# A second buffer for the tiles that the DMA turns, and v's loads, squares and parts moved between blocks

## The chip, the cores and the metric

The kernel runs on one core of a Trainium2 chip. The metric is the device time of one execution in microseconds (us), given as the median of several runs. An engine is named as in the profile: PE multiplies, ACT (ScalarE) and DVE (VectorE) work on whole tiles, POOL does one addition per pair of heads, and SP issues nearly all DMAs from one queue, in order.

## What is computed

Attention with a sigmoid in place of the softmax for 8 batches of 12 heads (448 tokens, 64 numbers per head), and behind it a two-layer network on the 3584 tokens:

```python
scores = scale * np.matmul(q, k.transpose(0, 1, 3, 2)) - np.log(S)
attn = 1.0 / (1.0 + np.exp(-scores))
attn_out = np.matmul(attn, v)
x = attn_out.transpose(0, 2, 1, 3).reshape(B * S, H * D)
h = x @ w_in
g = h - np.tanh(h)
return g @ w_out
```

## The kernel before

**Number format.** From batch 1 on, q and k, and from batch 2 on v and the sigmoids too, are split into two float16 parts, high and low, after a scaling by a power of two; a product is then three PE passes (high-high, high-low, low-high). The scaling needs the sum of squares of q, k and v for two pairs of heads: `norm` (lines 311 to 316) squares a tile on ACT and adds it up, throwing the squares into a junk tile of tag "sq"; `scales` (lines 318 to 345) makes the factors.

**Two stages per batch.** For each batch the first layer (`moe1`, line 746) is a dense run of PE products. The second layer (`moe2`, line 855) has 48 steps of 6 products (line 874) over three token tiles of 128 (16 steps each), then a rest of 64 tokens (line 912). Between its steps the attention of the next batch is fed in, in blocks, by the numbers in `BLOCKS` (8, 12, 16, ... 52): after that many steps, one block. At the end of a token tile (steps 16, 32, 48) the two accumulators leave PSUM, one on ACT (line 903, tile `o`), one on DVE (line 904). There are two PSUM buffers for them, so PE can't begin the next token tile before both are copied out.

**The blocks.** `stream` (lines 450 to 611) yields four blocks per two pairs of heads, g and h = g + 1:
- block 1 (lines 574 to 583): the first two score tiles of g, the products attention times v (`do_av`) of the pair before, v's parts of h (`prep_v(h)`), the loads of q and k of g+3 and of v of g+3, and the squares of v of g+2;
- block 2 (585 to 591): the remaining score tiles of g, the split of their sigmoids (`keep`, which calls `split_a`, lines 399 and 400), the squares of q, k and v of g+3;
- block 3 (593 to 599): the factors for g+2 and g+3, the first score tiles of h, and the parts of k and q of g+2 (`parts_k`, `parts_q`);
- block 4 (601 to 609): the last score tile of h, the parts of k and q of g+3, v's parts of g+2, the load of v of g+4, and the squares of q and k of g+4.

With `BLOCKS`, block 4 comes at steps 8, 24 and 40, block 1 at 12, 28 and 44, block 2 at 16, 32 and 48, right behind the evacuation of a token tile, and block 3 at 20, 36 and 52.

**The turned tiles.** `parts` (lines 347 to 361) writes the two float16 parts of k or q into a tile `w` (line 351) and has the DMA turn it into `K` or `Q` (line 358, issued on SP). For q the high part is written by ACT (line 353) and the low part by DVE (line 356); for k both are written by DVE (lines 355 and 356). `w` has one buffer: whoever writes the next `w` waits for the DMA that reads the one before. In the order of the program the four `w` of two pairs are k of g+2, q of g+2, k of g+3, q of g+3.

**What sets the order.** The order of PE, ACT, DVE and POOL is that in which the code is written. The DMAs on SP are put in order by a scheduler, which may issue a load ahead of the place where the code asks for it. Each engine takes its instructions in order, so one that waits holds up all behind it.

**The staged weights.** While w_in is converted at the start, `conv_norm` (line 159) writes squares of its pieces into tiles of tag "sq" of which four are in flight, and `conv_end` (line 170) sums four at a time on PE.

Of the kernel before, what the change touches and what calls it, by code (L numbers as in the profile page):

```python
# [8 lines left out]
F16 = mybir.dt.float16  # L9
BF16 = mybir.dt.bfloat16  # L10
# [9 lines left out]
P = 128  # L20
D = 64
CK = 112
# [12 lines left out]
class Builder:  # L35
# [123 lines left out]
    def conv_norm(self, p):  # L159
        nc = self.nc  # L160
        k = p["k"]
        if not p["staged"]:
            return
        p["sq"] = self.sm.tile([P, p["piece"][3]], BF16, name="sq", tag="sq", bufs=4)
        if k % 6 == 1:
            nc.vector.scalar_tensor_tensor(p["sq"], p["F"], 1.0, p["F"], op0=ALU.mult, op1=ALU.mult)
        else:
            nc.scalar.activation(p["sq"], p["F"], AF.Square)
# [142 lines left out]
    def norm(self, t, out):  # L311

        flat = t.rearrange("p a b d -> p (a b d)" if len(t.shape) == 4 else "p a d -> p (a d)")
        rows, n = flat.shape
        junk = self.sm.tile([P, 8 * D], BF16, name="sqn", tag="sq", bufs=4)
        self.nc.scalar.activation(junk[:rows, :n], flat, AF.Square, accum_out=out[:rows])  # L316

    def scales(self, ss, where):
# [28 lines left out]
    def parts(self, n, s, name, act):  # L347

        nc = self.nc
        flat = n.rearrange("p c h d -> p (c h d)")  # L350
        w = self.qk.tile([CK, 2, 4 * P], F16, name="w", tag="w", bufs=1)
        if act:
            nc.scalar.activation(w[:, 0], flat, AF.Copy, scale=s[:CK])  # L353
        else:
            nc.vector.tensor_scalar(w[:, 0], flat, s[:CK], None, op0=ALU.mult)
        nc.vector.scalar_tensor_tensor(w[:, 1], flat, s[:CK], w[:, 0], op0=ALU.mult, op1=ALU.subtract)  # L356
        o = self.qk.tile([P, 2, self.S], F16, name=name, tag=name)
        nc.sync.dma_start_transpose(
            o.rearrange("p x (c t) -> p (x c) t", c=4), w.rearrange("p x e -> p (x e)")
        )  # L360
        return o
# [88 lines left out]
    def stream(self):  # L450

        NP = self.NP
        G = (self.B - 1) * NP
        at = lambda g: (1 + g // NP, g % NP)
        splits = lambda g: at(g)[0] >= self.AV32
        qk, vn, sc, K, Q, vv, accs = {}, {}, {}, {}, {}, {}, {}

        def load(g):
            if g < G and g not in qk:
                qk[g] = self.load_qk(*at(g))

        def load_v(g):
            if g < G and splits(g):
                vn[g] = self.load_v(*at(g), self.nat, "vn", 2)

        def sums(g):
            ss = self.sums[g // 2 % 2]  # L470
            return ss if splits(g) else ss[:, :4]

        def norms(g):
            if g < G:
                for n, t in enumerate(qk[g]):
                    self.norm(t, sums(g)[:, 2 * n + g % 2 : 2 * n + g % 2 + 1])

        def norm_v(g):
            if g in vn:
                self.norm(vn[g], sums(g)[:, 4 + g % 2 : 5 + g % 2])  # L480

        def scales(g, where):
            if g < G:
                sc[g] = sc[g + 1] = self.scales(sums(g), where)

        def parts_k(g):
            if g < G:
                K[g] = self.parts(qk[g][0], sc[g][0][:, 0:1], "K", not splits(g) and g not in (2, 3))

        def parts_q(g):  # L490
            if g < G:
                Q[g] = self.parts(qk[g][1], sc[g][0][:, 1:2], "Q", True)
                qk.pop(g)

        def prep_v(g):
            if g >= G:
                return
            if splits(g):
                vv[g] = self.prep_v(vn.pop(g), sc[g][0])
            else:  # L500
                vv[g] = self.load_v(*at(g), self.att, "vhl", 3)[:, None]

        load(0)
        load(1)
        yield 0, False
        norms(0)
        norms(1)
        yield 0, False
        scales(0, "tr")
        parts_k(0)  # L510
        yield 450, False
        parts_q(0)
        load(2)
        yield 450, False
        parts_k(1)
        yield 450, False
        parts_q(1)
        load(3)
        yield 450, False
        norms(2)  # L520
        yield 0, False
        todo = []

        def open_acc(g):
            tag = "tr" if g % 2 else "av"
            accs[g] = self.ps.tile([P, 512], F32, name="acc", tag=tag, bufs=1)
            if g % NP == 0:
                self.xs = []

        def close_acc(g):  # L530
            iv = sc[g][1][:, 1:2] if splits(g) else None
            self.xs.append(self.evac_x(g % NP, accs.pop(g), iv))
            if g % 2:
                vv.pop(g - 1)
                vv.pop(g)
            for d in (sc, K, Q):
                d.pop(g)

        def do_av():
            for g, c, A in todo:  # L540
                odd = g % 2
                if c == QT:
                    open_acc(g + 1)
                    self.av([accs[g], accs[g + 1]], vv[g], A, c, odd)
                    close_acc(g)
                    continue
                if c == 0 and not odd:
                    open_acc(g)
                self.av([accs[g]], vv[g], A, c, odd)
                if c == QT - 1 and odd:  # L550
                    close_acc(g)
            todo.clear()

        def units(g, cs, between=lambda: None):

            pss = []
            for c in cs:
                n = 2 if c == QT else 1
                pss.append(self.scores([K[g + i] for i in range(n)], [Q[g + i] for i in range(n)], c))
            aa = [self.weigh(pss[0], sc[g][1][:, 0:1])]  # L560
            between()
            aa += [self.weigh(ps, sc[g][1][:, 0:1]) for ps in pss[1:]]
            return aa

        def keep(g, cs, aa):
            if splits(g):
                aa = [self.split_a(a) for a in aa]
            todo.extend((g, c, a) for c, a in zip(cs, aa))

        for g in range(0, G, 2):  # L570
            h = g + 1
            early = not splits(g)

            aa = units(g, (0, 1))
            do_av()
            if g == 0:
                prep_v(0)
            prep_v(h)
            keep(g, (0, 1), aa)
            load(g + 3)  # L580
            load_v(g + 3)
            norm_v(g + 2)
            yield 2750, True

            aa = units(g, (2, QT))
            if early:
                do_av()
            keep(g, (2, QT), aa)
            norms(g + 3)
            norm_v(g + 3)  # L590
            yield 2750, True

            scales(g + 2, "sc" if early else "av")
            aa = units(h, (0, 1), lambda: parts_k(g + 2))
            do_av()
            keep(h, (0, 1), aa)
            parts_q(g + 2)
            load(g + 4)
            yield 2750, True

            aa = units(h, (2,), lambda: parts_k(g + 3))
            if early:
                do_av()
            keep(h, (2,), aa)
            parts_q(g + 3)
            prep_v(g + 2)
            load_v(g + 4)
            norms(g + 4)
            yield 2750, True
        do_av()  # L610
        yield 1150, True
# [454 lines left out]
```

## Time and profile before

| | |
|---|---|
| time, median of 3 runs | 1353.88 us (1351.56 to 1355.76) |
| profiled execution, its own time | 1343.7 us |
| its span, from first to last instruction | 1341.4 us |
| mean granted PE clock | 0.958 of full speed |
| ACT busy, DVE busy | 902.5 us (67%), 910.6 us (68%) |
| SP's DMA queue, share of 16 DMA engines | 27.6% |

A row of a timeline gives the start of an instruction (or of several alike, "x24") in us from the beginning of the span, how long it lasted, its engine, its line, what it writes and reads, and in brackets how long the engine had stood idle before it and what ended that. A row of "windows" gives for a stretch of time how long each engine was busy in it and which share of the full PE clock was granted. A matmul's end is modelled, so a PE that is shown as busy can still run at a lower clock. Batch 3's second layer, with the attention of batch 4 in it, lies between 673.5 and 773.7 us; the other batches look alike, but the last has no attention to feed in, and the one before it less.

### The profile page before, as it was taken

How to read it: one execution, taken by the hardware profiler on the slowest of the kernel's cores; microseconds unless marked ns; L12 is line 12 of the kernel's file. 1: busy time of each engine (PE TensorE's matmuls, PEld its weight loads, DVE VectorE, ACT ScalarE, POOL GpSimd, SP SyncE). 2: the span in 40 equal slices, each digit the busy share in tenths (PEclk: the TensorE clock that was granted, in tenths of full speed). 3: DMA queues.
4: the chain of work that ended last, by engine and by line, in shares of the span. 5: the costliest groups of instructions: out<-in, count | busy, mean ns of one | idle time of the engine just before them, and what ended most of it. 6: DMA issues, size and time to landing. Idle time of an engine off the chain costs nothing.

```text
span 1341.4 us, 19713 instructions
## 1 busy us (share of the span) xinstructions
PE 1220.2 (91%) x7633; PEld 622.4 (46%) x7633; DVE 910.6 (68%) x1376; ACT 902.5 (67%) x1262; POOL 37.9 (3%) x38
## 2 busy tenths in 40 slices
PE   9899767799888899889998899888998999899998
PEld 3244323355444455445544455444544455445555
DVE  5999866579744688457964679546974579644940
ACT  6767765668866587666876668666876768752830
POOL 0100000000000000000000000000000000010000
PEclk9999888899988999989999999999998899999999
DMA  9953275210043300432023310333013320210000
GB/s 255 263 151 90 51 185 142 51 48 1 17 90 79 85 8 20 91 88 52 0 54 81 81 35 0 81 89 80 1 34 88 83 46 1 60 34 19 1 12 30
DMA packets 225678, 89.77 MB, mean 67 GB/s; under 512 B 213936, under 2 KB 215728, under 8 KB 225584
## 3 DMA queue, kind: packets, MB, share of 16 engines
q1 hardware_dynamic: 224656, 88.28, 27.6%
q8 instruction: 60, 0.98, 0.3%
q10 hardware_dynamic: 928, 0.23, 0.1%
q14 instruction: 34, 0.28, 0.1%
HBM read 58.20 MB, written 11.01 MB: 52 GB/s over the span
## 4 chain that ended last, share of the span: by engine, by line
PE 55%; DMA 6%; ACT 6%; DVE 3%; issue 2%; SPq 1%; ACTq 0%; DVEq 0%
PE ph L759 24%; PE po L874 21%; PE sc L382 4%; PE acc L413 3%; PE por L912 3%; DMA K<-w 2%; DMA vn<-v 2%; ACT a L393 2%; ACT sqn L316 2%; DMA kn<-k 1%; DVE ahl L400 1%; ACT ahl L399 1%; DVE vhl L368 1%; ACT o L903 1%; SPq L297 1%
## 5 line engine op out<-in xcount | busy, mean ns | idle before, releaser
L874 PE MATMUL po<-wo,g 128*128 128x384 f16 x2304 | 419.8, 341 | 48.9 <-ACT o L903 39.9
L759 PE MATMUL ph<-xhl,wi 128*128 128x448 f16 x2016 | 382.6, 352 | 0.0
L874 PEld LDWEIGHTS <-g 128*128 128x128 f16 x2304 | 229.0, 101 | 252.7 <-issue 123.0
L759 PEld LDWEIGHTS <-wi 128*128 128x128 f16 x2016 | 196.7, 98 | 185.0 <-issue 1.8
L400 DVE SCALAR_TENSOR_TENSOR ahl<-a,ahl 128x896 f16<-128x896 f32 x126 | 137.6, 1125 | 129.9 <-ACT ahl L399 129.8
L393 ACT ACTIVATE a<-sc,nls,rn 128x896 f32<-128x896 f32 x147 | 154.5, 1089 | 30.9 <-PE sc L382 24.2
L382 PE MATMUL sc<-Q,K 64*128 64x448 f16 x1008 | 113.5, 376 | 22.6 <-ACT tn L329 9.6
L829 ACT ACTIVATE u<-ph,ih 128x896 f32<-128x896 f32 x64 | 64.4, 1006 | 84.1 <-PE ph L759 79.4
L353 ACT ACTIVATE w<-qn,sn 112x512 f16<-112x512 f32 x42 | 30.1, 716 | 125.0 <-DMA K<-w 125.0
L399 ACT ACTIVATE ahl<-a 128x896 f16<-128x896 f32 x126 | 113.2, 940 | 0.8 <-DVE m L847 0.2
L833 DVE SCALAR_TENSOR_TENSOR m<-ph,ihk,u 128x896 f32<-128x896 f32 x64 | 73.5, 1148 | 38.8 <-ACT th L831 38.3
L356 DVE SCALAR_TENSOR_TENSOR w<-qn,sn,w 112x512 f16<-112x512 f32 x42 | 31.8, 757 | 88.2 <-ACT w L353 62.6
L743 ACT ACTIVATE g<-m,Sg 128x896 f16<-128x896 f32 x64 | 66.7, 1042 | 36.1 <-DVE m L847 30.9
L847 DVE COPY_PREDICATED m<-u,th 128x896 f32<-128x896 uint32 x64 | 77.5, 1211 | 6.6
L413 PE MATMUL acc<-ahl,vhl 128*64 128x448 f16 (+1 forms) x864 | 81.8, 359 | 0.0
L382 PEld LDWEIGHTS <-K 64*128 64x128 f16 x1008 | 39.7, 101 | 89.7 <-issue 68.1
L744 DVE SCALAR_TENSOR_TENSOR g<-m,Sg,g 128x896 f16<-128x896 f32 x64 | 73.4, 1146 | 8.8 <-ACT g L743 8.8
L844 DVE SCALAR_TENSOR_TENSOR m<-q,m 128x896 f32<-128x896 f32 x64 | 69.9, 1092 | 10.5 <-ACT q L843 3.4
L789 PE MATMUL ph<-x,wi 128*128 128x448 f32 x192 | 75.1, 540 | 0.2 <-DVE x L425 0.2
L834 DVE SCALAR_TENSOR_TENSOR th<-ph,ih,th 128x896 f32<-128x896 f32 x64 | 73.2, 1145 | 0.0
L846 ACT ACTIVATE u<-u,b 128x896 f32<-128x896 f32 x64 | 66.7, 1042 | 7.3 <-DVE m L833 5.4
L840 DVE SCALAR_TENSOR_TENSOR m<-q,m 128x896 f32<-128x896 f32 x64 | 69.5, 1086 | 0.0
(132 smaller groups left out, 1201.1 us busy)
## 6 DMA issues: line engine op xcount, KB each, us to landing
raw<-moe_w_in SPq DMA_DIRECT2D x24, 512.0 KB, 5.3
rawo<-moe_w_out SPq DMA_DIRECT2D x32, 384.0 KB, 3.9
kn<-k SPq DMA_DIRECT2D x96, 112.0 KB, 2.9
qn<-q SPq DMA_DIRECT2D x94, 112.0 KB, 2.9
vn<-v SPq DMA_DIRECT2D x96, 96.0 KB, 2.6
out<-o SPq DMA_DIRECT2D x21, 384.0 KB, 2.3
vn<-v SPq DMA_DIRECT2D x48, 32.0 KB, 2.4
out<-orem SPq DMA_DIRECT2D x16, 96.0 KB, 2.2
```

What stands on the lines that cost most here:

```text
L382: self.nc.tensor.matmul(ps[i * m : (i + 1) * m, h, : self.S], K[i][r, w, c * P : c * P + m], Q[i][r, x, :], start=(n == 0), stop=(n == len ...
L393: self.nc.scalar.activation(a[:, 0], ps[:, :, : self.S], AF.Sigmoid, bias=self.nls, scale=scale)
L399: nc.scalar.activation(A[:, 0], a[:, 0], AF.Copy, scale=A_SCALE)
L400: nc.vector.scalar_tensor_tensor(A[:, 1], a[:, 0], A_SCALE, A[:, 0], op0=ALU.mult, op1=ALU.subtract)
L413: self.nc.tensor.matmul(acc[i][h * D : (h + 1) * D, : self.S], v[k, w, 2 * QT + h if half else h * QT + c], A[k, x, h], start=(n == 0 and ...
L744: nc.vector.scalar_tensor_tensor(g[:, 1], m, Sg, g[:, 0], op0=ALU.mult, op1=ALU.subtract)
L759: nc.tensor.matmul(ph[:, e, :S], self.wi[:, c * self.NB + k, part, e * P : (e + 1) * P], xhl[c][:, x, :], start=(i == 0), stop=(i == 3 * s ...
L789: nc.tensor.matmul(ph[:, e, :S], self.where("in", c)[:, f * P : (f + 1) * P], xs[c], start=(c == 0), stop=(c == self.NC - 1),)
L833: V.scalar_tensor_tensor(m, ps, ihk, u, op0=ALU.mult, op1=ALU.mult)
L834: V.scalar_tensor_tensor(th, ps, ih, th, op0=ALU.mult, op1=ALU.subtract)
L847: V.copy_predicated(m, u.bitcast(U32), th)
L874: nc.tensor.matmul(po[i][:, :H], gs[f // 2][:, x, f % 2, tk * P : (tk + 1) * P], self.wo[:, i * self.NF + f, w], start=(f == 0 and n == 0) ...
```

## The change

```diff
@@ conv_norm
-        p["sq"] = self.sm.tile([P, p["piece"][3]], BF16, name="sq", tag="sq", bufs=4)
+        pool, tag = (self.qk, "w") if k % 2 else (self.sm, "sq")
+        p["sq"] = pool.tile([P, p["piece"][3]], BF16, name="sq", tag=tag, bufs=2)
@@ norm
-        junk = self.sm.tile([P, 8 * D], BF16, name="sqn", tag="sq", bufs=4)
+        junk = self.sm.tile([P, 8 * D], BF16, name="sqn", tag="sq", bufs=2)
@@ parts
-        w = self.qk.tile([CK, 2, 4 * P], F16, name="w", tag="w", bufs=1)
+        w = self.qk.tile([CK, 2, 4 * P], F16, name="w", tag="w", bufs=2)
@@ stream, block 1
             if g == 0:
                 prep_v(0)
-            prep_v(h)
+                prep_v(1)
             keep(g, (0, 1), aa)
             load(g + 3)
-            load_v(g + 3)
             norm_v(g + 2)
+            norm_v(g + 3)
@@ stream, block 2
             if early:
                 do_av()
+            norms(g + 3)
             keep(g, (2, QT), aa)
-            norms(g + 3)
-            norm_v(g + 3)
@@ stream, block 4
             prep_v(g + 2)
+            prep_v(g + 3)
             load_v(g + 4)
+            load_v(g + 5)
             norms(g + 4)
```

`w` gets a second buffer; the junk tile of the squares goes from four buffers to two, and the squares of w_in's pieces use these two and the two of `w` in turn. In the blocks, v's parts of g+3 and the load of v of g+5 move from block 1 back to the block 4 before it, the square of v of g+3 moves from block 2 to block 1, and the squares of q and k of g+3 move ahead of the splits within block 2. The lines of the changed kernel have numbers that are one higher at `parts` and two higher in `moe2`.

On ACT, blocks 1 and 2 around the evacuation of a token tile, before (`sqn` are the squares, `ahl` the high parts of the sigmoids `a32`, `o` the evacuation, `tn` the first step of `scales`):

```order
L399 ACTIVATE ahl_5484<-a32_5454 128x896
L316 ACTIVATE sqn_5496,ss0_112<-vn_5405 128x512
L903 ACTIVATE o_5541<-po0_5237,iK_4665 128x384
L393 ACTIVATE a32_5565<-sc_5545,nls_96,rn_5275 128x896
L393 ACTIVATE a32_5567<-sc_5552,nls_96,rn_5275 128x896
L399 ACTIVATE ahl_5569<-a32_5565 128x896
L399 ACTIVATE ahl_5572<-a32_5567 128x896
L316 ACTIVATE sqn_5575,ss0_112<-kn_5487 112x512
L316 ACTIVATE sqn_5577,ss0_112<-qn_5490 112x512
L316 ACTIVATE sqn_5579,ss0_112<-vn_5493 128x384
L329 ACTIVATE tn_5648<-pbn_5646,tiny_104 128x6
```

and the same place of the changed kernel:

```order
L400 ACTIVATE ahl_5487<-a32_5460 128x896
L317 ACTIVATE sqn_5496,ss0_112<-vn_5408 128x512
L317 ACTIVATE sqn_5498,ss0_112<-vn_5413 128x384
L905 ACTIVATE o_5543<-po0_5237,iK_4665 128x384
L394 ACTIVATE a32_5567<-sc_5547,nls_96,rn_5275 128x896
L394 ACTIVATE a32_5569<-sc_5554,nls_96,rn_5275 128x896
L317 ACTIVATE sqn_5571,ss0_112<-kn_5490 112x512
L317 ACTIVATE sqn_5573,ss0_112<-qn_5493 112x512
L400 ACTIVATE ahl_5575<-a32_5567 128x896
L400 ACTIVATE ahl_5578<-a32_5569 128x896
L330 ACTIVATE tn_5648<-pbn_5646,tiny_104 128x6
```

The square of the second v tile (128x384) now stands ahead of the evacuation, and the squares of k and q ahead of the two splits.

On SP, the DMAs from the k parts of g+3 (block 4) to the store of the evacuated token tile, before (`K`, `Q` are the turned tiles, `kn`, `qn`, `vn` the loads):

```order
L358 DMA_TRANSPOSE K_8530<-w_8527 128x8x112
L286 DMA kn_8625<-k 112x4x64 x2
L358 DMA_TRANSPOSE Q_8538<-w_8535 128x8x112
L286 DMA qn_8628<-q 112x4x64
L297 DMA vn_8543<-v 128x3x64 x2
L301 DMA vn_8543<-v 64x2x64 x2
L286 DMA qn_8628<-q 112x4x64
L297 DMA vn_8631<-v 128x3x64 x2
L867 DMA out<-o_8679 128x768
```

and in the changed kernel:

```order
L359 DMA_TRANSPOSE K_8530<-w_8527 128x8x112
L287 DMA kn_8628<-k 112x4x64 x2
L359 DMA_TRANSPOSE Q_8538<-w_8535 128x8x112
L287 DMA qn_8631<-q 112x4x64
L298 DMA vn_8546<-v 128x3x64 x2
L302 DMA vn_8546<-v 64x2x64 x2
L298 DMA vn_8551<-v 128x3x64 x2
L287 DMA qn_8631<-q 112x4x64
L869 DMA out<-o_8681 128x768
```

The second v load passes one half of a q load, and in the first two pairs of a batch both halves; nothing else moves here. In batch 0 the loads of w_out, k and v on SP change places among each other and the q parts move ahead of some of them. DVE's order changes in one place only, also in batch 0, where v's second parts move ahead of nine splits of w_in; PE's and POOL's orders stay the same.

## Prediction

> **What bounds the kernel now.** I read the page's engines first, then the sums of waits, then the stages, then one batch row by row.
>
> ```profile
> span 1341.4 us, 19713 instructions
> PE 1220.2 (91%) x7633; PEld 622.4 (46%) x7633; DVE 910.6 (68%) x1376; ACT 902.5 (67%) x1262; POOL 37.9 (3%) x38
> ```
>
> PE is busy for 91% of the span, so only what stops or slows PE can be won. The sums of waits give the largest of both kinds:
>
> ```profile
> ACT w L353 <- DMA K<-w: 125.0, 27, 6.6
> PE po L874 <- ACT o L903: 39.9, 14, 4.4
> ```
>
> ACT stands 125 us in front of the q parts, because the only `w` is still being read by the DMA that turns k; PE stands 39.9 us until ACT has evacuated `o`. ACT works in order, so the first may cause the second. Where it happens, the windows by stage show (batch 0's second layer, then batches 1 to 6; the last of the right-hand numbers but two is the granted PE clock, ahead of the DMA share):
>
> ```profile
> core 0: us, PE busy (x) PEld busy (x) DVE busy (x) ACT busy (x) POOL busy (x), PEclk, DMA share, GB/s
> 180.00:290.00 110.00, 86.80 (x556) 41.85 (x554) 78.12 (x175) 76.22 (x152) 4.67 (x4) 0.91 0.43 110
> 290.00:463.00 173.00, 153.36 (x1033) 79.01 (x1032) 115.89 (x173) 123.54 (x173) 4.53 (x4) 0.94 0.22 49
> 463.00:619.00 156.00, 144.81 (x968) 75.69 (x966) 106.11 (x151) 110.37 (x150) 4.53 (x4) 0.96 0.24 54
> 619.00:774.00 155.00, 144.59 (x972) 75.57 (x971) 106.23 (x151) 110.37 (x150) 4.53 (x4) 0.97 0.24 54
> 774.00:928.00 154.00, 142.78 (x966) 74.67 (x965) 105.29 (x151) 110.36 (x150) 4.53 (x4) 0.97 0.24 54
> 928.00:1084.00 156.00, 144.96 (x974) 75.53 (x970) 106.22 (x151) 110.49 (x150) 4.53 (x4) 0.96 0.24 54
> 1084.00:1225.00 141.00, 134.58 (x891) 72.52 (x889) 92.09 (x121) 89.11 (x108) 4.53 (x4) 0.98 0.15 33
> ```
>
> PE's loss in a stage is its idle time and what the lowered clock takes (one less the granted share, times the length). That is 33 us in batch 0 (23.2 + 9.9), 30.0 in batch 1 (19.6 + 10.4), then 17.4, 15.1, 15.8, 17.2, and 9.2 in batch 6. Batches 2 to 5 lose 16.4 us each on average; batches 1 to 6 together lose 104.7. No more than this can be won there. Batch 3 stands for them; its PE rows:
>
> ```profile
> 697.88 5.74 PE L874 MATMUL po<-wo,g 128*128 128x384 f16 x24 [2.47 <-ACT o L903]
> ...
> 719.18 4.07 PE L874 MATMUL po<-wo,g 128*128 128x384 f16 x24
> ...
> 724.65 0.76 PE L382 MATMUL sc<-Q,K 64*64 64x448 f16 x10 [0.18 <-DMA Q<-w]
> 729.13 5.74 PE L874 MATMUL po<-wo,g 128*128 128x384 f16 x24 [3.73 <-ACT o L903]
> ...
> 736.16 2.58 PE L413 MATMUL acc<-ahl,vhl 128*64 128x448 f16 x30
> ...
> 754.34 0.36 PE L686 MATMUL nm<-x2b,onesb 128*128 128x448 bf16 x1 [0.82 <-ACT a L393]
> 756.51 0.35 PE L686 MATMUL nm<-x,onesb 128*128 128x448 bf16 x1 [1.81 <-ACT x L438]
> 756.70 1.96 PE L874 MATMUL po<-wo,g 128*128 128x384 f16 x6
> ...
> 760.81 4.09 PE L912 MATMUL por<-wo,g 128*64 128x384 f16 x48
> 765.56 0.39 PE L327 MATMUL pbn<-ss,onesf 128*128 128x6 f32 x2 [0.66 <-ACT sqn L316]
> ```
>
> The stops lie behind the ends of the three token tiles: site A (697.88), site B (729.13), site C (754.34 to 765.56). After A and B the same 24 products take 5.74 us where they otherwise take 4.07: the stop costs another 1.67 us of clock. Now ACT ahead of B:
>
> ```profile
> 713.35 0.95 ACT L399 ACTIVATE ahl<-a 128x896 f16<-128x896 f32 x1
> 720.12 0.72 ACT L353 ACTIVATE w<-qn,sn 112x512 f16<-112x512 f32 x1 [5.82 <-DMA K<-w]
> ...
> 721.97 2.07 ACT L393 ACTIVATE a<-sc,nls,rn 128x896 f32<-128x896 f32 x2
> ...
> 727.89 0.63 ACT L316 ACTIVATE sqn<-vn 128x512 bf16<-128x512 f32 x1 [0.98 <-DMA vn<-v]
> 728.52 0.56 ACT L903 ACTIVATE o<-po,iK 128x384 f32<-128x384 f32 x1
> ```
>
> The evacuation at 728.52 stands behind v's squares, these wait for v's load, and everything from 720.12 on stands behind the wait of 5.82 us. SP and DVE in the same stretch, and how long a turn takes from issue to landing:
>
> ```profile
> 712.69 1.22 SPq L358 DMA_TRANSPOSE Q<-w  x1
> 713.95 1.14 SPq L286 DMA_DIRECT2D qn<-q  x2
> 717.06 1.22 SPq L358 DMA_TRANSPOSE K<-w  x1
> ...
> 721.65 1.54 SPq L358 DMA_TRANSPOSE Q<-w  x1
> ...
> 724.92 1.29 SPq L301 DMA_DIRECT2D vn<-v  x2
> 726.26 0.59 SPq L286 DMA_DIRECT2D qn<-q  x1
> 726.95 0.97 SPq L297 DMA_DIRECT2D vn<-v  x2
> ```
>
> ```profile
> 711.92 0.74 DVE L356 SCALAR_TENSOR_TENSOR w<-qn,sn,w 112x512 f16<-112x512 f32 x1
> 715.72 0.49 DVE L355 TENSOR_SCALAR w<-kn,sn 112x512 f16<-112x512 f32 x1 [3.06 <-issue]
> ```
>
> ```profile
> K<-w SPq DMA_TRANSPOSE x2, 3.0
> ```
>
> It is a chain through one buffer: Q turned at 712.69, landed 3.0 later, k's parts at 715.72, K turned at 717.06, landed 3.0 later, q's parts at 720.12, Q turned at 721.65, and v's loads stand behind it on SP.
>
> **The second `w`, site B.** K's parts no longer wait for Q: DVE goes on at 712.7 and ends 1.2 later at 713.9. SP is free at 715.1 (713.95 + 1.14), so K is turned 2 us earlier. Q's parts wait only for the Q before, landed at 715.7 instead of 720.1; ACT ends them at 716.4, DVE at 717.2. SP needs 1.22 for K and some 1.14 for two k loads, so Q is issued at 717.5: 4.1 us earlier than 721.65, and with it v's loads. What is late next is v's landing.
>
> **The second v square ahead of `o`.** Its load is issued behind the first (724.92 and 726.95); with the q load between them (0.7 us) gone behind, the last halves lie some 1.2 us apart. So it starts 1.2 after the first square and takes about 0.7 where `o` used to start 0.63 after it: `o` comes 1.2 us later. Net, `o` is 2.9 us earlier at B and PE resumes at 726.2. Its scores end at 725.2 (724.65 + 0.76, less the wait of 0.18), so a stop near 1 us stays. I take the clock as kept: 2.9 + 1.67 = 4.6 us.
>
> Site A has slack of its own on the buffer:
>
> ```profile
> 686.06 1.26 SPq L358 DMA_TRANSPOSE K<-w  x1
> ...
> 690.66 1.22 SPq L358 DMA_TRANSPOSE Q<-w  x1
> ```
>
> K stays; SP reaches Q behind K and two k loads at 688.5, 2.1 us earlier; both q loads now stand behind v, 0.7 more; less 1.2 for the second square: 1.6 us. About 1 us of stop stays, preceded by scores that wait; I count half of the clock: 2.4 us. At C, the waits of 0.82 and 1.81 end on ACT, which is 4 us earlier, so they go, and so does the slow clock of the next six products (1.96 against 1.02, a quarter of 4.07); the 0.66 at 765.56 goes as well, since the second v square is done by then: 4.2 us. Batches 2 to 5: 4 x 11.2 = 45 us, 68% of the loss.
>
> A rule weighs on the clock. The Trainium skill, "TensorE: Matmul & The Clock Gate", section "HAM oscillation — how this bites in real kernels", says that PE is throttled by idle gaps above about 3.4 us. The trace disagrees at A: 2.47 us was enough. By the rule a stop of 1 us is surely harmless, and the four sites A would give 0.8 us more each, 3 us in all.
>
> **The squares of q and k ahead of the splits** (block 2). Between the start of `w` at 720.12 and the sigmoids at 721.97 lie `w` with 0.72 and these squares, so 1.2 us; the splits come that much later. What hides it:
>
> ```profile
> 731.93 2.09 DVE L400 SCALAR_TENSOR_TENSOR ahl<-a,ahl 128x896 f16<-128x896 f32 x2 [3.02 <-ACT ahl L399]
> ```
>
> The splits end at 734.0; the products at 736.16 read them after the first 12 of 30, at 737.2. Of 3.2 us of cover, 1.67 goes with the clock and 1.2 with the move: 0.3 us is left. If that is gone too, up to 1 us per site is lost.
>
> **At no cost.** The junk tiles of `norm` are written by ACT alone and read by nobody, so two suffice; the staged squares keep four tiles in flight, two and two. DVE has v's parts in the same order as before. The load of v is issued at the same place on SP, but for a q load: moving it in the code brings next to nothing beyond that 0.7 us. If `w`'s earlier turns crowd the DMA engines, the cover is their share of 0.24 in these stages.
>
> **Batches 6, 1 and 0.** Batch 6 at the same 68% of 9.2: 6 us. Batch 1 has closer blocks and waits for Q that stay, so less than 68% of 30: 17. In batch 0 ACT and DVE also convert and split weights, and SP's order changes; I see nothing there that prices it. Bounds are 0 (ACT stays the bound) and 14 (42% of 33); I take 9, nearer to the upper end, since the same wait for K stands there.
>
> **Sum.** 45 + 6 + 17 + 9 = 77 us. The profiled execution took 1343.7 us in all, so 1267; the runs' median is 1353.88, 10 us above it, and I take the same 77 off: 1277.
>
> **Rivals.**
> - *Everything flows better* (0.16): the earlier blocks feed the next ones, 80% of the 104.7 goes, and 14 in batch 0: 98 us, 1256. For it: PE's own work leaves no other stop. Against: v's landing still ends last at A and B.
> - *The stops shrink, the clock stays low* (0.15): A 1.6, B 2.9, C 2.6, so 28 for four batches, 4 and 11 for batches 6 and 1 in proportion, nothing in batch 0: 43 us, 1311. For it: gaps of 0.82 and 1.81 did lower the clock at C.
> - *No gain* (0.03): the evacuation is bound by the landing of v whatever `w` does, since SP is held by another wait; 1354.
> - *Slower, by the second v square* (0.04): it now stands ahead of `o` at some 16 token ends. If Q is issued less than 1.2 us earlier, because turns and loads crowd on one queue, each of them costs up to 1.2 us: 19 us, 1373. Against: DVE and SP stood free from 715.1 on.
>
> **How the numbers follow.** The forecast has 0.62. The range goes from the better rival to a little beyond the weak one, 1256 to 1315. A measurement of this kernel tells about 0.3% from no change. Faster 0.93, the same 0.03, slower 0.04.
>
> **What would show it.** After: ACT's wait for K at line 353 nearly gone, what is left of it on Q's DMA; Q issued about 4 us sooner behind the last scores of h; two v squares in a row ahead of `o`, the second waiting on its load; PE's wait for `o` down from 39.9 to some 15 us; the granted clock at 0.97 or more in batches 1 to 5; no stop at `nm`. I am wrong if PE's wait for `o` stays above 30 us, if it waits for the splits in block 3, or if SP holds Q back.

## The result, and the profile after

The changed kernel takes 1290.21 us (median of 4 runs, 1281.98 to 1292.20) against 1352.77 (4 runs, 1351.56 to 1355.76) of the kernel before: a ratio of 0.9523, 95% interval 0.9477 to 0.9568. It is faster by 62.6 us where 77 were forecast, inside the range. The profiled execution took 1281.98 us, with a span of 1279.7.

The page's engines after, and then the sums of waits (engine, what it was about to write, line, what released it: us in total, times, longest):

```profile
span 1279.7 us, 19703 instructions
PE 1190.1 (93%) x7633; PEld 618.1 (48%) x7633; DVE 908.4 (71%) x1376; ACT 902.2 (70%) x1262; POOL 37.9 (3%) x38
```

```profile
PE po L876 <- ACT o L905: 28.8, 13, 4.1
...
PE por L914 <- ACT o L905: 6.0, 7, 1.8
PE sc L383 <- DVE m L690: 4.5, 5, 1.5
PE pbn L328 <- ACT sqn L317: 4.3, 2, 3.4
```

```profile
ACT sqn L317 <- DMA vn<-v: 33.7, 30, 2.9
...
ACT w L354 <- DMA Q<-w: 20.6, 13, 2.4
```

ACT's wait of 125.0 us for K's turn is gone; what is left in front of the q parts ends on Q's DMA and is 20.6 us. But PE's wait for the evacuation `o` has only come down from 39.9 to 28.8, and ACT now stands 33.7 us, 30 times, in front of v's squares.

The windows of the stages of batches 2 to 5 after, in the columns that the prediction's windows have:

```profile
441.00:590.00 149.00, 141.08 (x966) 75.32 (x966) 105.55 (x150) 110.15 (x151) 4.54 (x4) 0.98 0.27 57
590.00:737.00 147.00, 140.78 (x978) 75.24 (x975) 106.67 (x152) 111.23 (x152) 4.54 (x4) 0.99 0.26 57
737.00:884.00 147.00, 139.99 (x971) 74.97 (x969) 105.67 (x151) 110.38 (x151) 4.54 (x4) 0.99 0.28 57
884.00:1030.00 146.00, 139.85 (x969) 74.89 (x968) 105.51 (x151) 110.28 (x151) 4.54 (x4) 0.99 0.28 58
```

These stages took 621 us before (463 to 1084) and take 589 now. Of these 32 us, 15.4 are PE's busy time, which fell from 577.1 to 561.7 for the same products at a better clock, and 16.6 are its idle time, from 43.9 to 27.3.

In batch 3 (590 to 737), PE behind the two token tiles A and B and around C:

```profile
668.62 5.74 PE L876 MATMUL po<-wo,g 128*128 128x384 f16 x24 [2.56 <-ACT o L905]
...
697.73 4.06 PE L876 MATMUL po<-wo,g 128*128 128x384 f16 x24 [2.36 <-ACT o L905]
...
723.44 0.76 PE L383 MATMUL sc<-Q,K 64*64 64x448 f16 x12 [0.97 <-DVE m L690]
...
724.52 4.09 PE L914 MATMUL por<-wo,g 128*64 128x384 f16 x48 [0.32 <-ACT o L905]
```

The stops at A and B are 2.56 and 2.36 us where some 1 us was forecast. A still loses the clock (5.74 us for 24 products), B keeps it (4.06). What ACT does ahead of them:

```profile
665.57 0.63 ACT L317 ACTIVATE sqn<-vn 128x512 bf16<-128x512 f32 x1 [1.91 <-DMA vn<-v]
...
667.49 0.52 ACT L317 ACTIVATE sqn<-vn 128x384 bf16<-128x384 f32 x1 [1.20 <-DMA vn<-v]
...
668.01 0.56 ACT L905 ACTIVATE o<-po,iK 128x384 f32<-128x384 f32 x1
...
695.54 0.63 ACT L317 ACTIVATE sqn<-vn 128x512 bf16<-128x512 f32 x1 [1.03 <-DMA vn<-v]
...
696.59 0.52 ACT L317 ACTIVATE sqn<-vn 128x384 bf16<-128x384 f32 x1 [0.33 <-DMA vn<-v]
...
697.11 0.56 ACT L905 ACTIVATE o<-po,iK 128x384 f32<-128x384 f32 x1
```

ACT stands 1.91 us for the first v tile at A and 1.20 for the second, at B 1.03 and 0.33, with `o` behind both. SP in the same stretch:

```profile
657.50 1.26 SPq L359 DMA_TRANSPOSE K<-w  x1
...
660.05 1.22 SPq L359 DMA_TRANSPOSE Q<-w  x1
661.37 1.09 SPq L298 DMA_DIRECT2D vn<-v  x2
662.50 1.39 SPq L302 DMA_DIRECT2D vn<-v  x2
663.99 1.28 SPq L298 DMA_DIRECT2D vn<-v  x2
...
685.96 1.22 SPq L359 DMA_TRANSPOSE K<-w  x1
688.58 1.23 SPq L359 DMA_TRANSPOSE Q<-w  x1
```

Q now follows K after 2.55 us at A and 2.62 at B, where it followed after 4.60 and 4.59 before. V's loads still stand behind Q, as before the change.

### The profile page after: what moved, and what is told of

The parts are those of the page before. It is cut to its first block, busy times and chain, and to the rows that moved or that the text cites. A ratio compares the mean times of both kernels' runs of the same rounds, so it can differ in the third digit from the quotient of the medians.

```text
span 1279.7 us, 19703 instructions
## 1 busy us (share of the span) xinstructions
PE 1190.1 (93%) x7633; PEld 618.1 (48%) x7633; DVE 908.4 (71%) x1376; ACT 902.2 (70%) x1262; POOL 37.9 (3%) x38
## 4 chain that ended last, share of the span: by engine, by line
PE 55%; DVE 13%; ACT 13%; DMA 9%; issue 6%; SPq 4%; DVEq 0%; ACTq 0%
PE ph L761 29%; PE po L876 12%; PE por L914 5%; PE acc L414 5%; DMA qn<-q 3%; PE sc L383 3%; ACT a L394 3%; DMA Q<-w 2%; SPq L298 2%; DVE ahl L401 2%; DMA rawo<-moe_w_out 1%; ACT sqn L317 1%; DVE m L835 1%; ACT ahl L400 1%; DVE m L849 1%
## 5 line engine op out<-in xcount | busy, mean ns | idle before, releaser
L876 PE MATMUL po<-wo,g 128*128 128x384 f16 x2304 | 402.6, 332 | 30.7 <-ACT o L905 28.8
L876 PEld LDWEIGHTS <-g 128*128 128x128 f16 x2304 | 223.6, 99 | 212.7 <-issue 75.9
L383 PE MATMUL sc<-Q,K 64*128 64x448 f16 x1008 | 104.3, 361 | 21.0 <-ACT tn L330 8.8
L745 ACT ACTIVATE g<-m,Sg 128x896 f16<-128x896 f32 x64 | 66.6, 1041 | 39.2 <-DVE m L849 33.7
L383 PEld LDWEIGHTS <-K 64*128 64x128 f16 x1008 | 36.9, 98 | 80.9 <-issue 58.8
L914 PE MATMUL por<-wo,g 128*64 128x384 f16 x768 | 64.9, 327 | 6.0 <-ACT o L905 6.0
L841 ACT ACTIVATE q<-u,b 128x896 f32<-128x896 f32 x64 | 65.8, 1029 | 0.0
```

The lines of the kernel that those rows point to most:

```text
L383: self.nc.tensor.matmul(ps[i * m : (i + 1) * m, h, : self.S], K[i][r, w, c * P : c * P + m], Q[i][r, x, :], start=(n == 0), stop=(n == len ...
L876: nc.tensor.matmul(po[i][:, :H], gs[f // 2][:, x, f % 2, tk * P : (tk + 1) * P], self.wo[:, i * self.NF + f, w], start=(f == 0 and n == 0) ...
L914: nc.tensor.matmul(po[e * D : (e + 1) * D, :H], gs[f // 2][:, x, f % 2, nm:S], self.wo[:, e * self.NF + f, w], start=(f == 0 and n == 0), ...
```

## Experiments

My theory after the result: the second buffer of `w` carries the whole gain, and the moves take part of it back, because two squares that wait for v's load now stand ahead of the evacuation on which PE waits. The rivals: the moves are needed for the gain; or v's landing doesn't matter, since something else holds the evacuation. Every time below is a median, with the ratio to the kernel before on the same chip and its 95% interval. The runs stand on four chips, on which the kernel before had medians from 1349.95 to 1353.94; between kernels of different chips the ratios count, and the differences of medians agree with them to 3 us.

**The changed kernel again**, as the measure for the others.

> The changed kernel once more, on the chip of the experiments beside it, so that these are compared with it there. Both theories: 1282 to 1292 us, as before; PE's wait for the evacuation near 29 us in 13 or 14 stops.

1290.15 us, ratio 0.9529 (0.9493 to 0.9565).

**The buffers alone.** `conv_norm`, `norm` and `parts` as changed, the blocks of `stream` as before.

```diff
-        w = self.qk.tile([CK, 2, 4 * P], F16, name="w", tag="w", bufs=1)
+        w = self.qk.tile([CK, 2, 4 * P], F16, name="w", tag="w", bufs=2)
```

> The second buffer of the turned tile and the buffers of the squares as in the change, the order of the blocks as before. Theory (the buffer is the whole gain; the second v square ahead of the evacuation takes some of it back): within 0.7% of the changed kernel, 1281 to 1299 us: the evacuation comes 1 to 1.8 us sooner at some 15 token ends, and the product of the sums of squares waits up to 1.6 us for the squares that again stand behind the splits. Rival (the moves between the blocks carry a good part of the gain): above 1315 us. PE's wait for the evacuation: near 15 us by the theory, above 30 by the rival.

1278.32 us, ratio 0.9456 (0.9427 to 0.9485): 74 us faster than before, and 12 faster than the change, a little more than my theory gave. The buffers of the squares change together with `w` in every run, so a part of their own isn't measured. The sums of PE's waits for the squares and for the evacuation in this kernel:

```profile
PE pbn L328 <- ACT sqn L317: 21.4, 16, 3.4
PE po L875 <- ACT o L904: 15.0, 13, 2.5
```

With one v square ahead of `o`, PE waits 15.0 us for it instead of 28.8. In return the squares of k, q and the second v tile, which stand behind the splits again, are late for the sums (`pbn`) of the factors: 21.4 us instead of 4.3.

**The moves alone.** `w` with one buffer, "sq" with four, the blocks as changed.

```diff
-        w = self.qk.tile([CK, 2, 4 * P], F16, name="w", tag="w", bufs=2)
+        w = self.qk.tile([CK, 2, 4 * P], F16, name="w", tag="w", bufs=1)
```

> The moves between the blocks as in the change, one buffer for the turned tile as before. Theory: no gain, 1345 to 1375 us; ACT's wait for K at the q parts stays near 125 us, and the evacuation stands behind two v squares instead of one, which costs 1 to 2 us at some 15 token ends, less what the earlier squares of q, k and v save ahead of the sums (up to 8 us in all). Rival (the moves carry part of the gain): 1315 to 1340 us.

1365.84 us, ratio 1.0100 (1.0069 to 1.0132): 14 us slower than before. The sums of waits have all of the old wait, and more of PE's:

```profile
ACT w L353 <- DMA K<-w: 130.5, 30, 7.5
...
PE po L875 <- DVE o L905: 38.5, 12, 3.6
...
PE po L875 <- ACT o L904: 16.7, 14, 2.4
```

The two waits of PE belong to the same stops, as site A of batch 3 shows:

```profile
704.40 0.32 PE L875 MATMUL po<-wo,g 128*128 128x384 f16 x1 [3.39 <-DVE o L905]
706.64 6.39 PE L875 MATMUL po<-wo,g 128*128 128x384 f16 x23 [1.92 <-ACT o L904]
```

DVE copies its accumulator at 703.74 and lets one product go; ACT's `o` follows only at 706.03, behind the second v square, where before the change the two started 0.04 us apart (697.31 and 697.27). Together PE waits 55.2 us for the evacuation here.

So the buffer is the cause of the gain, and the moves cost 14 us without it and 12 with it.

**Both v squares behind the evacuation.** Out of block 1, into block 2 behind the squares of q and k.

```diff
             load(g + 3)
-            norm_v(g + 2)
-            norm_v(g + 3)
             yield 2750, True
...
             norms(g + 3)
+            norm_v(g + 2)
+            norm_v(g + 3)
             keep(g, (2, QT), aa)
```

> The changed kernel with both v squares moved from block 1 to block 2, behind the squares of q and k and ahead of the splits, so that the evacuation no longer stands behind them. Theory (v's load, 5.5 to 7 us behind the issue of Q, ends last at the token ends of the changed kernel): PE's wait for the evacuation falls from 29 to below 8 us, the clock no longer falls behind it, 1250 to 1272 us. Rival (the evacuation would be held by something else, or the splits, 1.4 us later, stop PE in block 3 instead): 1282 us or more, with a new wait of the products attention times v for the splits.

1255.89 us, ratio 0.9290 (0.9260 to 0.9319). PE's waits:

```profile
PE pbn L328 <- ACT sqn L317: 11.1, 9, 4.0
...
PE po L876 <- ACT o L905: 4.1, 4, 2.2
```

With no square that waits for a load ahead of it, the evacuation is hardly a limit any more: 4.1 us, and 3.3 for DVE's half. This is 34 us faster than the changed kernel on the same chip.

**The second v square alone behind it.** Only `norm_v(g + 3)` is moved to block 2, behind `norms(g + 3)` and ahead of `keep`.

```diff
             norm_v(g + 2)
-            norm_v(g + 3)
             yield 2750, True
...
             norms(g + 3)
+            norm_v(g + 3)
             keep(g, (2, QT), aa)
```

> The changed kernel with only the second v square moved from ahead of the evacuation to block 2, behind the squares of q and k and ahead of the splits. Theory (each v square ahead of the evacuation costs by its load's landing; the first one alone leaves the stop that the buffer alone showed, and the squares ahead of the splits spare the wait of the sums, 21 us there): PE's wait for the evacuation near 15 us, its wait for the sums below 8 us, 1262 to 1272 us. Rival (the second square matters only with the first; or the wait for the sums comes back in another place): 1276 us or more.

1259.80 us, ratio 0.9330 (0.9297 to 0.9362), a little better than expected. PE's waits:

```profile
PE po L876 <- ACT o L905: 13.6, 13, 2.1
...
PE pbn L328 <- ACT sqn L317: 5.1, 3, 3.4
```

The second square costs the changed kernel 0.0199 of 1352, some 27 us. The two profiled spans, 1279.7 and 1252.7, differ by the same 27. Of it, 15.2 are PE's wait for `o` (28.8 less 13.6), and some 7 the clock: 0.980 of 1279.7 us granted loses 25.6, 0.985 of 1252.7 loses 18.8. The waits of `por` and of `sc` on `m` are smaller by 4.3.

**All squares of block 2 last.** Both v squares and those of q and k behind `keep`.

```diff
-            norms(g + 3)
             keep(g, (2, QT), aa)
+            norms(g + 3)
+            norm_v(g + 2)
+            norm_v(g + 3)
```

> Both v squares in block 2 as in the best run so far, but all squares of block 2 behind the splits. Theory: no wait for the evacuation, but the sums wait for the squares at every token end, some 2 us at 15 places, so PE's wait for the sums 25 to 40 us and 1272 to 1292 us. Rival (the splits are what PE needs first in block 3, so their delay and not the sums' counts): 1256 us or less.

1267.36 us, ratio 0.9394 (0.9367 to 0.9421). PE's waits:

```profile
PE pbn L328 <- ACT sqn L317: 27.7, 17, 4.0
...
PE po L876 <- ACT o L905: 3.0, 3, 2.0
```

The evacuation is free, and the factors are late instead: 27.7 us against 11.1 with the squares ahead of the splits. Even so it is faster than the changed kernel, and 5 us below my range.

**Both v squares later, with one `w`.** The kernel with both v squares behind the evacuation, but with `w` in one buffer and "sq" in four.

> The best run so far (both v squares in block 2, ahead of the splits) with one buffer for the turned tile, as in the kernel before. Theory (both faults act on one chain: one buffer keeps ACT waiting for K, near 125 us, and the splits and sigmoids ahead of the evacuation stay late, only the wait for v's load and the squares themselves go): 1315 to 1340 us. Rival (the place of the squares was the fault alone, and the buffer is worth little once they are out of the way): 1285 us or less.

1335.19 us, ratio 0.9890 (0.9860 to 0.9921). ACT waits for K's turn as long as in the moves alone (134.2 and 130.5 us).

By the ratios the squares' place is worth 28 us with one buffer (1.0100 less 0.9890) and 32 with two (0.9529 less 0.9290); the buffer is worth 77 with the squares ahead of the evacuation and 81 with them behind it. Within the intervals, some 6 us on each difference, the two are independent terms, not one chain in which the second only shows once the first is gone.

**The squares of q and k behind the splits.** The changed kernel with this one move taken back.

```diff
-            norms(g + 3)
             keep(g, (2, QT), aa)
+            norms(g + 3)
```

> The changed kernel with the squares of q and k in block 2 put back behind the splits; both v squares stay ahead of the evacuation. Theory (PE reads the splits with some 0.3 us to spare and the sums at once, so the squares belong ahead; but v's squares are already out of this place, so less than with the buffer alone is left to wait for): PE's wait for the sums 5 to 15 us, 1288 to 1302 us. Rival (the splits that come later were themselves a cost of the change): 1284 us or less.

1302.97 us, ratio 0.9649 (0.9619 to 0.9679): slower than the changed kernel by 0.0120, some 16 us (13 by the medians). PE's waits:

```profile
PE po L876 <- ACT o L905: 33.7, 13, 4.2
...
PE pbn L328 <- ACT sqn L317: 9.4, 7, 2.9
```

So of the moves this one is a gain. PE's waits here are 3.4 to 4.9 us more for `o` and 5.1 to 6.0 more for the sums than in the changed kernel's two profiles (28.8 and 30.3; 4.3 and 3.4); the granted clock is 0.969, there 0.980 and 0.971. The trace doesn't tell which of these is cause and which is effect.

**No landing of v to wait for.** The squares of v read tiles of k that landed earlier, of the same width (112x512 and 112x384 for 128x512 and 128x384); v's own sum of squares is left out of the computation.

```diff
-                self.norm(vn[g], sums(g)[:, 4 + g % 2 : 5 + g % 2])
+                t = qk[g - g % 2][0]
+                t = t[:, :QT] if g % 2 else t
+                self.norm(t, sums(g)[:, 4 + g % 2 : 5 + g % 2])
```

> The changed kernel, but the two squares in front of the evacuation read k of the even pair, which landed long before, in place of the two v tiles: the same work on ACT at the same place without the wait for v's load. So the factor for v is taken from k's squares and v's own sum is left out. Theory (the landing of v's loads ends last at the token ends, not ACT's own time): PE's wait for the evacuation below 15 us instead of 29, ACT's wait for v gone, 1260 to 1275 us. Rival (ACT's time for two squares, 1.4 us, is what delays the evacuation): 1282 us or more, with a wait above 22 us.

1243.49 us, ratio 0.9185 (0.9163 to 0.9207). PE's waits:

```profile
PE po L878 <- ACT o L907: 4.7, 4, 2.1
...
PE pbn L328 <- ACT sqn L317: 5.2, 3, 3.4
```

ACT does as many squares of the same length (0.61 and 0.51 us) in the same places, v's loads stand where they stood on SP, and the time is 47 us lower than the changed kernel's, lower than I had expected: it is the landing, not the squares' own time, that costs. I had expected the kernel below, with both squares behind the evacuation, to be the faster of the two, and missed: without a landing to wait for, PE's wait for `o` is 4.7 us even with two squares ahead of it, and PE's wait for the sums is 5.2 us against 11.1 and 11.5 in the two profiles of that kernel. Whether the place ahead of `o` is the better one in itself isn't shown, since no kernel has squares without a landing behind it.

**Two repeats on the same chip as that**: both v squares later,

> Both v squares in block 2, once more, to stand on the same chip as the kernel beside it. Both theories: 1252 to 1260 us, so 3 to 20 us below the kernel with the squares of k, whose evacuation still stands behind 1.4 us of ACT.

1255.25 us, ratio 0.9262 (0.9236 to 0.9289), and the second alone later,

> Only the second v square back in block 2, once more, on the same chip as the kernel with both. Theory (the first square's wait for its load is what is left): 2 to 8 us above the kernel with both in block 2. Rival (the wait of the sums that the other kernel has instead weighs as much): no difference that the intervals show.

1258.21 us, ratio 0.9295 (0.9273 to 0.9317). They lie 3 us apart with overlapping intervals; which is better stays open. Both are 12 to 15 us behind the kernel without the landing.

**V's loads ahead of the turns.** The whole computation, with v's parts (`prep_v`) of g+2 and g+3 and the loads of v of g+4 and g+5 moved from block 4 to the end of block 3.

```diff
@@ end of block 3
+            prep_v(g + 2)
+            prep_v(g + 3)
+            load_v(g + 4)
+            load_v(g + 5)
             yield 2750, True
@@ block 4
             parts_q(g + 3)
-            prep_v(g + 2)
-            prep_v(g + 3)
-            load_v(g + 4)
-            load_v(g + 5)
             norms(g + 4)
```

> The changed kernel, complete, but v's parts of g+2 and g+3 and the loads of v of g+4 and g+5 move on from block 4 to the end of block 3, so that SP issues v's loads ahead of the turns of k and q of g+3 and not behind them. Theory (the landing of v's loads is all that holds the evacuation): ACT's wait for v nearly gone, PE's wait for the evacuation below 10 us, 1240 to 1255 us, so close to the kernel with the squares of k. Rival (v's parts, 2.3 us of DVE, now delay the turns of k and q of g+3, and PE waits for these in block 2): 1265 us or more, with a new wait of the scores for Q.

1238.12 us (6 runs, 1234.93 to 1239.16), ratio 0.9150 (0.9126 to 0.9174): the fastest of all, and 2 us below my range. PE is busy for 96% of the span. PE's waits, and SP ahead of site A of batch 3:

```profile
PE sc L383 <- DMA Q<-w: 4.9, 5, 1.7
...
PE po L876 <- ACT o L905: 1.0, 2, 0.5
```

```profile
662.85 0.97 SPq L298 DMA_DIRECT2D vn<-v  x2
663.87 1.39 SPq L302 DMA_DIRECT2D vn<-v  x2
665.35 1.07 SPq L298 DMA_DIRECT2D vn<-v  x2
666.53 1.26 SPq L359 DMA_TRANSPOSE K<-w  x1
667.89 1.24 SPq L359 DMA_TRANSPOSE Q<-w  x1
```

V's loads now stand ahead of the last K and Q of the two pairs, 5 us before that Q. ACT behind them:

```profile
670.92 0.61 ACT L317 ACTIVATE sqn<-vn 128x512 bf16<-128x512 f32 x1
...
671.53 0.51 ACT L317 ACTIVATE sqn<-vn 128x384 bf16<-128x384 f32 x1
...
672.04 0.56 ACT L905 ACTIVATE o<-po,iK 128x384 f32<-128x384 f32 x1
```

Both squares run without a wait, and `o` follows 1.12 us after the first instead of 2.44. PE waits 1.0 us for `o` in the whole run, and 4.9 for Q, 3.0 in the changed kernel: the rival's wait is small. The run moves v's parts along with the loads and doesn't separate the two; the kernel without the landing, which moves neither, is some 5 us slower.

## Why the prediction was right, and where it was off

**The buffer.** Right. The wait for K is gone, the rest is on Q's DMA, and Q is issued about 2.6 us behind K, close to the 2.4 worked out (two loads and a turn). The kernel with the buffers alone shows that this is the whole gain, and the moves alone show that it isn't theirs: the rival that the evacuation is bound by v's landing "whatever `w` does" falls. Half of it was true: once the buffer is open, the landing is what holds the evacuation.

**The sum by stages.** Measured from the first product of each batch's first layer (line 759 before, 761 after) to the next:

| | forecast | measured |
|---|---|---|
| up to batch 1 (290.09, then 282.19) | 9 | 7.9 |
| batch 1 (172.75, then 158.88) | 17 | 13.9 |
| batches 2 to 5 (621.28, then 588.59) | 45 | 32.7 |
| batch 6 (141.48, then 134.29) | 6 | 7.2 |
| all, with the last stage | 77 | 61.7 |

Three of the four terms are off by 1 to 3 us; of the 15 us that are missing, 12 are those of batches 2 to 5, where the 11.2 us for each measured 8.2. The changed kernel's second profile, with a span of 1290.2, gives 4.6, 12.1, 29.3 and 5.2 for the four, so a term moves by 2 to 3 us from run to run. The 9 of batch 0 was a choice between two bounds with no mechanism behind it: that it came out near is luck.

**The step that failed** is "so a stop near 1 us stays" at A and B. The eight stops of batches 2 to 5 in the trace after run from 1.75 to 2.84 us and sum to 19.5, so 2.44 each; three of the eight kept the clock, where I had counted six. It failed from two sides, which the rows of batch 3 show when all is counted from Q's issue:

- *The evacuation came later.* At A, PE resumed 8.57 us after Q's issue (668.62 less 660.05), where I had 7.8 (696.3 less 688.5): ACT waited 1.20 us for the second load, and the second square started 1.92 behind the first instead of 1.2. At B it is 9.15 against 8.7.
- *PE came sooner.* PE had run out of work at 666.06 (668.62 less the stop of 2.56), 6.0 us after Q's issue where the working had 6.8 (7.8 less the stop of 1); at B at 695.37, 6.8 after, where it had 7.7. I had moved ACT and SP forward and left PE's arrival where it stood, though each stop that shrinks brings PE sooner to the next.

Together 1.6 us at A and 1.4 at B: that is the difference between a stop of 1 us and the stops seen.

Which side weighs more shows when all is counted from the batch's first product (619.01 before, 590.49 after):

| sooner than before, us | A, forecast | A, measured | B, forecast | B, measured |
|---|---|---|---|---|
| Q's issue | 2.1 | 2.1 | 4.1 | 4.6 |
| PE resumes behind `o` | 1.6 | 0.7 | 2.9 | 2.9 |
| PE runs out of work | 0 | 0.8 | 0 | 1.5 |

So Q came as forecast or better. At B the evacuation did too, and the whole miss is PE's arrival; at A it is half and half. PE came sooner at A because its scores no longer wait for Q. Before, they did:

```profile
694.65 0.76 PE L382 MATMUL sc<-Q,K 64*64 64x448 f16 x10 [0.46 <-DMA Q<-w]
```

After, all 18 products there run in one piece from 664.63. At B half of the 1.5 us comes from A's earlier end, and the rest from scores that no longer wait (before, 0.18 for Q and 0.16 for the sigmoids) and run in one piece.

**The second v square ahead of `o`.** I priced it at 1.2 us a site and let it stand as a small term in a gain. Its direct price was about right: where it is taken back, PE's wait for `o` falls by 15.2 us over 11 places, 1.4 each (two more, of 0.51 us in the last batch, stay). But 1.4 us on top of a stop of about 1 reaches the lengths at which the clock can fall, and it hits nearly every token tile: some 27 us in all. I had this as a rival that would turn the change slower and gave it 0.04. As a sign it was wrong, because the buffer outweighs it; as a mechanism it was there, and larger than the 19 us that I set.

**The squares of q and k ahead of the splits.** Said to have 0.3 us of cover left and to cost up to 1 us a site if that goes. The splits aren't waited for by the products in the sums after; the move gains 13 to 16 us instead. In these two blocks I had looked only at who waits for the splits, not at who waits for the squares. Against the 27 us of the second v square this leaves 11 to 14 us, in line with the 12 that the moves cost together.

**The load of v, "moving it in the code brings next to nothing".** Right in the main, and this is where most of the time still lay: the second load is issued 3.9 us behind the last Q at A and 5.1 at B, 5.4 and 5.3 before, so 1.5 and 0.2 us closer where I had 0.7. The loads stay behind that Q, and the landing goes on costing 47 us. One block further, ahead of that K and Q, the same lines and v's parts bring 52.

**At C,** the waits of `nm` are gone but for 0.7 us, as said, and two small ones grew: 6.0 us of `por` on `o` in 7 stops (1.1 before), and 4.5 of scores on DVE's `m` in 5 (0.9 before).

**The signs named beforehand.** Q sooner behind the last scores of h (3.8 us at B, 2.1 at A, where I had named about 4), two v squares in a row with the second waiting on its load, no stop at `nm`, a clock of 0.97 or more: all there. PE's wait for `o` at some 15 us was not; 28.8, and 30.3 in the second profile of the same kernel, lie on both sides of the 30 from which I was to be wrong: the account of `o` had failed, though the time came out inside the range. It is 15.0 with the buffers alone.

**Open.** A third buffer for `w`, which might take ACT's remaining wait of 20.6 us for Q's DMA (as large in the fastest kernel, 20.4), wasn't tried. Why the squares of q and k behind the splits lengthen PE's wait for `o` too stays open. How the 7.9 us of batch 0 divide stays open.

## What to carry to other kernels

When a serial buffer is opened, price each other edit of the same change on its own: here the buffer brought 74 us and the moves beside it took 12 back. Don't put work that waits for a load ahead of an evacuation on an engine that works in order, or else bring the load forward in the DMA queue itself: moving its line brought at most 1.5 us of earlier issue while it stood behind the same turns, and with v's parts 52 us of time once it passed them. When a stop is forecast to shrink, move both ends of it, the one that releases and the one that arrives.

## What the runs showed of the hardware

The clock falls behind shorter stops than I had reckoned with, and not at one sharp length. Always the same 24 products, behind a stop for `o`: in the changed kernel's second profile,

```profile
554.13 4.06 PE L876 MATMUL po<-wo,g 128*128 128x384 f16 x24 [2.69 <-ACT o L905]
...
672.67 5.68 PE L876 MATMUL po<-wo,g 128*128 128x384 f16 x24 [2.52 <-ACT o L905]
```

and in the repeat of the kernel with the second v square alone later

```profile
515.65 5.74 PE L876 MATMUL po<-wo,g 128*128 128x384 f16 x24 [1.93 <-ACT o L905]
```

In all profiles of this case every single stop of up to 1.87 us at this place left the clock full (4.06 to 4.10 us) and every one from 2.71 us on lowered it (5.4 to 6.9 us); from 1.93 to 2.69 both are seen. Two short stops close together can do it as well: at site C before the change, 0.82 and 1.81 us; and in batch 6 before the change 0.85 and 1.22 us with one product between, behind which the other 23 took 5.58 us. In the kernel with the moves alone the same two stops, 0.85 and 1.22, left the 23 at 3.90. The Trainium skill, "TensorE: Matmul & The Clock Gate", section "HAM oscillation — how this bites in real kernels", puts the limit at idle gaps above about 3.4 us. These rows differ from it: 1.93 us was enough once. So a term of a forecast that hangs on a stop between 1.9 and 2.7 us is best counted at half its price.
